# Router logits of three token chunks by row products on VectorE

## The chip, the cores and the metric

One of the eight cores of a Trainium2 chip runs the whole program: TensorE (matrix products), VectorE, ScalarE and GpSimd work on the on-chip memory, and SyncE (SP) issues most of the transfers. Each engine takes its instructions in a fixed order and waits on semaphores for the others. The metric is the time of one execution in microseconds (us), as the device counts it.

## What is computed

Attention of two kinds (on averaged keys and in a local band) over 4 batches, 8 heads, 576 positions and 64 dimensions is added and laid out as 2304 tokens of 512 numbers. A gated feed-forward layer of width 1536 follows, and then a layer of eight experts, of which each token takes one. The part that the change touches, from the reference:

```python
xn = x / (np.linalg.norm(x, axis=-1, keepdims=True) + 1e-06)
en = expert_emb / (np.linalg.norm(expert_emb, axis=-1, keepdims=True) + 1e-06)
logits = xn @ en.T / tau
expert_idx = np.argmax(logits, axis=1)
...
gate_w = probs[np.arange(N), expert_idx]
for e in range(E):
    h = np.maximum(x[mask] @ w1[e], 0.0)
    out[mask] = gate_w[mask, None] * (h @ w2[e])
```

Here `x` is the output of the gated layer, 2304 x 512, and there are 8 embeddings of 512 numbers.

## The kernel before

**Tiling.** The 2304 tokens are worked in nine chunks of 256, each chunk as two tiles of 128 rows (`m` = 0 and 1). For each chunk the gated layer runs over six blocks `p` of 256 hidden units. In a block, TensorE forms gate and value (L963: groups of 24 products with 256 columns), ScalarE the tanh, VectorE the gating (L914, L916) and the low part (L921), and TensorE adds the block to the chunk's output (L995: 512 columns) in a PSUM bank per tile. Every full-precision product is made as three products of high and low parts. While a block's output products run, the next block's or chunk's L963 products stand around them.

**Routing.** When the last block of a chunk is added, `route(c)` and `route_m(c, m, ...)` send the tokens to their experts. For each tile: the row is copied out of PSUM (L1032), its sum of squares formed on ScalarE (L1035), the row transposed in four pieces on TensorE (L1040), copied (L1045), and multiplied with the transposed embeddings `enT` to eight logits per token (L1050), in a PSUM bank `lp`. GpSimd forms the root of the norm (L1058). For both tiles together VectorE scales the logits (L1090), takes maximum and index (L1093, L1095) and writes one-hot rows `oh` (L1097); TensorE counts ranks with them (L1104, L1105), VectorE makes slots (L1108 to L1116), and GpSimd scatters token number and gate weight into the table `tab` (L1123). All of this runs while TensorE already works on the next chunk's L963 products.

**Experts.** Each expert has up to 336 slots in three tiles. The slot table is loaded (L1239, L1244 on SP), the rows gathered (L1258 on GpSimd), transposed on TensorE (L1268), and multiplied with the expert's two layers (L1312, L1322). The first two tiles of expert 0 are gathered before the last chunk is routed, the others after it. The experts' weights are loaded by SP (L1214, L1217) and split into high and low parts (L1197 on ScalarE, L1200 on VectorE).

**Preparation.** `prep_en` loads the eight embeddings (L457), normalises them on VectorE (L468), transposes them on TensorE and leaves them as `enT` (L473). The weights of the gated layer are loaded at L394 and decoded by L405, L413, L416 and L426.

**Order.** The program is written as many small generators. A list scheduler runs them against estimated durations and priorities and so fixes the order of each engine's instructions when the program is built; an instruction's position in its engine's queue depends on it. Tiles come from slot classes (`ps` PSUM banks, `t2` and `sg` rows, `aw` 4 KB-wide work tiles, `w` weights), and a slot that is given back is reused by whoever asks next.

Of the kernel before, what the change touches and what calls it, by code (L numbers as in the profile page):

```python
# [11 lines left out]
F32 = mybir.dt.float32  # L12
# [7 lines left out]
ALU = mybir.AluOpType  # L20
# [4 lines left out]
P = 128  # L25
B, H, S, D = 4, 8, 576, 64
HP = H // 2
DM = H * D
NTOK = B * S
FF = 1536  # L30
E = 8
# [8 lines left out]
NCHUNK = NTOK // CT  # L40
# [25 lines left out]
def t_dve(n): return 62 + 1.045 * n  # L66
# [180 lines left out]
HEAD_P = [0.0, 0.1, 0.2, 0.3, 1.4, 2.2, 3.2, 4.2, 16.0, 17.0, 18.0, 19.0, 36.0, 37.0, 38.0, 39.0]  # L247
NE = 8
EARLY_N = range(NE)
NV = 4  # L250
REST_P = 0.5
NSET = 3
# [4 lines left out]
def build(tc, a):  # L257
    nc = tc.nc
# [22 lines left out]
    def op(eng, ns, prio=None, how=None):  # L281
        return ("op", eng, ns, prio, how)
# [11 lines left out]
    def dma(n):  # L294
        return ("op", "DMA", t_dma(n), None, None)
# [24 lines left out]
    nc.scalar.dma_start(out=tau, in_=a["tau"].to_broadcast([P, 1]))  # L320
    enT = cst.tile([P, KD, E], F32, name="enT")
    x2d = dr.tile([NTOK, DM], F32, name="x2d")
    tab = dr.tile([E * EST, 4], I32, name="tab")
    ovc = cst.tile([P, 1], F32, name="ovc")
    ovm = cst.tile([P, 1], I32, name="ovm")
# [127 lines left out]
    def prep_en():  # L453
        ps = yield ("get", "ps")
        en, junk = t01[:E, 256:768], ps[:E, 0:DM]
        yield dma(E * 2048)
        nc.sync.dma_start(out=en, in_=a["emb"])  # L457
        ss = cst.tile([E, 4], F32, name="ess")
        yield op("ACT", t_act(DM))
        nc.scalar.activation(junk, en, AF.Square, accum_out=ss[:, 0:1])  # L460
        yield op("POOL", 530)
        nc.gpsimd.tensor_tensor(out=ss[:, 1:2], in0=ss[:, 0:1], in1=half[:E, 0:1], op=ALU.pow)
        yield op("DVE", 80, None, True)
        nc.vector.tensor_scalar(out=ss[:, 2:3], in0=ss[:, 1:2], scalar1=1e-6, scalar2=None, op0=ALU.add)
        yield op("DVE", 120)
        nc.vector.reciprocal(ss[:, 3:4], ss[:, 2:3])
        yield op("DVE", 350, None, True)
        nc.vector.tensor_scalar(out=en, in0=en, scalar1=ss[:, 3:4], scalar2=None, op0=ALU.mult)  # L468
        yield op("PE", 340)
        for k in range(KD):  # L470
            nc.tensor.transpose(ps[:, k * E:(k + 1) * E], en[:, k * P:(k + 1) * P], ident[:E, :E])
        yield op("DVE", 110)
        nc.vector.tensor_copy(enT, ps[:, 0:KD * E].rearrange("p (k e) -> p k e", k=KD))  # L473
        sc.put("ps", ps)
        sc.set("en")


    def pget(n=1):

# [545 lines left out]
    def route_m(c, m, sv, lp):  # L1025

        hi = -1.0
        row = yield ("get", "t2")
        yield ("wait", ("x2", c, m))
        xp = x2p.pop((c, m))  # L1030
        eng = yield psum(DM, hi)
        copy[eng](row, xp)  # L1032
        sc.spawn(sc.cur.prio, store_x2(c, m, row))
        yield op("ACT", t_actp(DM) + 110, hi)
        nc.scalar.activation(xp, xp, AF.Square, accum_out=sv[:, 0, m:m + 1])  # L1035
        sc.spawn(sc.cur.prio, route_norm(c, m, sv))
        yield ("lag", SLACK)
        for k in range(KD):
            yield op("PE", 108, hi)
            nc.tensor.transpose(xp[:, k * P:(k + 1) * P], row[:, k * P:(k + 1) * P], ident)  # L1040
        sc.set(("rowT", c, m))
        tcls = "w" if c == NCHUNK - 1 else "t2"
        x2T = last_T[m] if last_T else (yield ("get", tcls))
        eng = yield psum(DM, hi)
        copy[eng](x2T[:, 0:DM], xp)  # L1045
        sc.put(x2cls(c), xp)
        yield ("lag", SLACK)
        yield op("PE", 810, hi)
        for k in range(KD):
            nc.tensor.matmul(lp[:, m * E:(m + 1) * E], x2T[:, k * P:(k + 1) * P], enT[:, k, :],  # L1050
                             start=(k == 0), stop=(k == KD - 1))
        sc.put(tcls, x2T)
        sc.set(("lg", c, m))

    def route_norm(c, m, sv):
# [11 lines left out]
    def route(c):  # L1067
        hi = -1.0
        if c == NCHUNK - 1:
            for m in range(2):  # L1070
                last_T.append((yield ("get", "w")))
        if c > 0:
            yield ("wait", ("tab", c - 1))
        lgt = [gm.tile([P, 2, E], t, tag=nm, name=f"{nm}{c}") for nm, t in
               (("lg", F32), ("oh", F32R), ("t8", F32), ("mx", F32), ("mxi", U32))]
        lg, oh, t8, mx, mxi = lgt
        sv = gm.tile([P, 4, 2], F32, tag="sv", name=f"sv{c}")
        si = gm.tile([P, 2], I32, tag="si", name=f"si{c}")
        yield ("wait", ("x2", c, 0))
        lp = yield ("get", "ps")  # L1080
        for m in range(2):
            if c == NCHUNK - 1:
                sc.spawn(sc.cur.prio, route_m(c, m, sv, lp))
            else:
                yield from route_m(c, m, sv, lp)
        for m in range(2):
            yield ("wait", ("norm", c, m))
            yield ("wait", ("lg", c, m))
        yield op("DVE", 90, hi)
        nc.vector.tensor_tensor(out=lg, in0=lp[:, 0:2 * E].rearrange("p (m e) -> p m e", m=2), in1=b8(sv[:, 3, :]), op=ALU.mult)  # L1090
        for m in range(2):
            yield op("DVE", 75, hi)
            nc.vector.max(out=mx[:, m, :], in_=lg[:, m, :])  # L1093
            yield op("DVE", 150, hi)
            nc.vector.max_index(out=mxi[:, m, :], in_max=mx[:, m, :], in_values=lg[:, m, :])  # L1095
        yield op("DVE", 90, hi)
        nc.vector.tensor_tensor(out=oh, in0=iota8, in1=b8(mxi[:, :, 0]), op=ALU.is_equal)  # L1097
        sc.spawn(sc.cur.prio, route_gate(c, lg, mx, mxi))

        yield ("lag", SLACK)  # L1100
        yield op("PE", 140, hi)
        rp = lp[:, 2 * E:6 * E].rearrange("p (w m e) -> p w m e", w=2, m=2)
        ohf = oh.rearrange("p m e -> p (m e)")
        nc.tensor.matmul(lp[:, 2 * E:4 * E], tri, ohf, start=True, stop=True)  # L1104
        nc.tensor.matmul(lp[:, 4 * E:6 * E], ones, ohf, start=True, stop=True)  # L1105
        bm = lambda x: x.unsqueeze(1).to_broadcast([P, 2, E])
        yield op("DVE", 90, hi)
        nc.vector.tensor_tensor(out=t8, in0=rp[:, 0], in1=bm(base), op=ALU.add)  # L1108
        yield op("DVE", 80, hi)
        nc.vector.tensor_tensor(out=t8[:, 1, :], in0=t8[:, 1, :], in1=rp[:, 1, 0, :], op=ALU.add)  # L1110
        yield op("DVE", 90, hi)
        nc.vector.tensor_tensor(out=t8, in0=t8, in1=oh, op=ALU.mult)
        yield op("DVE", 90, hi)
        nc.vector.tensor_reduce(out=sv[:, 0, :], in_=t8, axis=AX.X, op=ALU.add)
        yield op("DVE", 90, hi, True)
        nc.vector.tensor_copy(si, sv[:, 0, :])  # L1116
        sc.set(("slot", c))
        sc.spawn(sc.cur.prio, route_base(c, lp, rp))
        yield ("wait", ("gate", c))
        for m in range(2):  # L1120
            yield ("lag", 1700 * m)
            yield op("POOL", 1010, hi)
            nc.gpsimd.indirect_dma_start(  # L1123
                out=tab[:, :], out_offset=bass.IndirectOffsetOnAxis(ap=si[:, m:m + 1].bitcast(U32), axis=0),
                in_=mt[:, 2 * c + m, :], in_offset=None, bounds_check=E * EST - 1, oob_is_err=False)
        yield ("lag", 2500)
        sc.set(("tab", c))
# [47 lines left out]
    def open_experts():  # L1175

        for k in range(HP):
            yield ("wait", ("x", NCHUNK - 1, k))
        at.__exit__(None, None, None)
        ep[0] = e2 = pool("e2")  # L1180
        slots("xh", e2, 2, [P, KD, CAP])
        slots("xl", e2, 2, [P, KD, CAP])
        slots("eh", e2, 2, [P, 2, CAP])
        slots("el", e2, 2, [P, 2, CAP])
        slots("xs", e2, 3, [P, DM])
        sc.set("experts")
# [310 lines left out]
    with tc.manual_schedule():  # L1497
        sc.spawn(0, x_slots(), 0.0)
        sc.spawn(0, x_split(1), 0.0)
        sc.spawn(0, fewer_banks(), 0.0)  # L1500
        for n in range(B * HP):
            sc.spawn(HEAD_P[n], heads(n), 0.0)
        sc.spawn(3, small_consts(), 0.0)
        sc.spawn(1000, keep_warm(), 0.0)
        sc.spawn(4, load_weights(), 0.0)
        sc.spawn(0.1, weight_slots(), 0.0)
        sc.spawn(3, prep_en(), 0.0)
        for c in range(NCHUNK):
            if c != 1:
                sc.spawn(c * 10 + 1, x_split(c), 0.0)  # L1510
        sc.spawn(5, gated(), 0.0)
        sc.spawn(NCHUNK * 10, open_experts(), 0.0)
        sc.spawn(NCHUNK * 10 + 4, load_experts(), 0.0)
        sc.spawn(NCHUNK * 10 + 1, all_slots(), 0.0)
        sc.run()
# [120 lines left out]
```

## Time and profile before

| | |
|---|---|
| median of three runs | 879.08 us (877.41 to 879.35) |
| the profiled execution | 879.53 us, of it the span 877.5 us |
| granted TensorE clock, mean | 0.99 |
| TensorE busy | 858.2 us (98%) |
| VectorE busy | 476.2 us (54%) |
| ScalarE busy | 381.2 us (43%) |
| GpSimd busy | 153.0 us (17%) |
| transfers | 88.10 MB, mean 100 GB/s |

The busy times are of one execution on the chip. TensorE's share says that little is left in which it stands; the views by stretch, by wait and by instruction say where that is. Lines are those of the kernel before. In the rows, PE is TensorE, DVE is VectorE, ACT is ScalarE, POOL is GpSimd; an arrow goes from what is read to what is written (`ps<-xhi,w` writes `ps`).

### The profile page before, as it was taken

To read this page: it belongs to the slowest core of one execution; us is meant where nothing else is said; L and a number is where in the kernel's file an instruction comes from. 1 tells how busy PE (TensorE), PEld (TensorE's weight loads), DVE (VectorE), ACT (ScalarE), POOL (GpSimd) and SP (SyncE) were. 2 spreads that over 40 slices of the span, in tenths; PEclk is the share of its full clock that TensorE was granted. 3 is DMA by queue.
4 is the path that set the end of the run, shared out by engine and by line. 5 is a ranking of instruction groups with operands and counts; after the bars stand their busy time and mean duration, and the time that the engine had idled before them with its cause. 6 is when DMAs were issued, how large, how long until landed. Compare 5 with 4: busy or idle time off the path is not lost. (4 is left out here: it accounts for less than half of the span.)

```text
span 877.5 us, 17216 instructions
## 1 busy us (share of the span) xinstructions
PE 858.2 (98%) x6976; PEld 768.3 (88%) x6977; DVE 476.2 (54%) x1132; ACT 381.2 (43%) x914; POOL 153.0 (17%) x163
## 2 busy tenths in 40 slices
PE   9989999999999999999999999999999999999995
PEld 4777889999999999999999999999888888888883
DVE  4799998566564365663342423666455544545210
ACT  3778788444342243341321313345354444445120
POOL 4443300022112010020010000201320330331111
PEclk9899999999999999999999999999999999999998
DMA  8593545102121021120000000453565554453100
GB/s 250 181 320 99 166 161 176 56 27 82 57 80 57 1 63 47 36 76 1 13 13 1 25 1 25 121 190 121 146 201 167 164 193 142 162 191 119 29 27 28
DMA packets 52627, 88.10 MB, mean 100 GB/s; under 512 B 7806, under 2 KB 24574, under 8 KB 52544
## 3 DMA queue, kind: packets, MB, share of 16 engines
q1 hardware_dynamic: 47664, 76.72, 27.8%
q0 software_dynamic: 4160, 9.48, 3.3%
q8 instruction: 55, 0.90, 0.4%
q10 hardware_dynamic: 720, 0.77, 0.3%
q14 instruction: 28, 0.23, 0.1%
HBM read 77.96 MB, written 10.57 MB: 101 GB/s over the span
## 5 line engine op out<-in xcount | busy, mean ns | idle before, releaser
L963 PE MATMUL ps<-xhi,w 128*128 128x256 f32 x1504 | 295.9, 288 | 1.7 <-POOL w L426 1.3
L963 PEld LDWEIGHTS ps<-xhi,w 128*128 128x128 f32 x1504 | 242.2, 191 | 5.4 <-POOL w L426 1.5
L963 PE MATMUL ps<-xlo,w 128*128 128x256 f32 x752 | 212.5, 283 | 0.0
L963 PEld LDWEIGHTS ps<-xlo,w 128*128 128x128 f32 x752 | 144.0, 191 | 1.4
L1312 PE MATMUL ps<-xh,w 128*128 128x336 f32 (+1 forms) x512 | 124.3, 315 | 0.0
L995 PE MATMUL x<-w,hh 128*128 128x512 f32 x384 | 120.8, 396 | 0.0
L914 DVE SCALAR_TENSOR_TENSOR th<-th,ps 128x256 f32<-128x256 f32 x108 | 45.1, 418 | 131.2 <-ACT th L912 130.8
L912 ACT ACTIVATE th<-ps 128x256 f32<-128x256 f32 x108 | 41.0, 380 | 137.4 <-PE ps L963 135.8
L1312 PEld LDWEIGHTS ps<-xh,w 128*128 128x128 f32 x512 | 88.3, 188 | 2.2
L1200 DVE TENSOR_TENSOR w<-w,w 128x1024 fp32r<-128x1024 f32 x64 | 76.6, 1217 | 22.2 <-ACT w L1197 22.1
L1312 PE MATMUL ps<-xl,w 128*128 128x336 f32 (+1 forms) x256 | 79.8, 312 | 0.0
L995 PEld LDWEIGHTS x<-w,hh 128*128 128x128 f32 x384 | 68.4, 189 | 12.2 <-issue 0.4
L1322 PE MATMUL x<-w,eh 128*128 128x512 f32 x248 | 78.0, 396 | 0.0
L995 PE MATMUL x<-w,hl 128*128 128x512 f32 x192 | 74.9, 390 | 0.0
L919 ACT CAST hh<-th 128x256 fp32r<-128x256 f32 x108 | 43.7, 405 | 68.8 <-DVE th L916 68.2
L1298 DVE SCALAR_TENSOR_TENSOR el<-ps,eh 128x336 fp32r<-128x336 f32 (+1 forms) x62 | 30.3, 493 | 79.1 <-ACT eh L1296 78.5
L1296 ACT ACTIVATE eh<-ps 128x336 fp32r<-128x336 f32 (+1 forms) x62 | 27.4, 442 | 90.0 <-PE ps L1312 84.6
L1197 ACT CAST w<-w 128x1024 fp32r<-128x1024 f32 x64 | 65.6, 1045 | 0.0
L1058 POOL TENSOR_TENSOR sv<-sv,half 128x1 f32<-128x1 f32 x18 | 10.4, 577 | 290.5 <-ACT x L1035 285.0
L921 DVE TENSOR_TENSOR hl<-th,hh 128x256 fp32r<-128x256 f32 x94 | 39.7, 424 | 30.9 <-ACT hh L919 30.8
L1322 PEld LDWEIGHTS x<-w,eh 128*128 128x128 f32 x248 | 45.4, 188 | 9.4
L1337 POOL DMA_INDIRECT out<-sg,tb x23 | 23.3, 1012 | 172.3 <-ACT sg L1329 160.7
(257 smaller groups left out, 1391.5 us busy)
## 6 DMA issues: line engine op xcount, KB each, us to landing
w<-w SPq DMA_DIRECT2D x64, 512.0 KB
w<-w_gate SPq DMA_DIRECT2D x10, 512.0 KB
w<-w_val SPq DMA_DIRECT2D x10, 512.0 KB
w<-w_out SPq DMA_DIRECT2D x10, 512.0 KB
w<-qk SPq DMA_DIRECT2D x16, 291.0 KB
aw<-qk SPq DMA_DIRECT2D x16, 291.0 KB
x2d<-sg SPq DMA_DIRECT2D x18, 256.0 KB
w<-vw SPq DMA_DIRECT2D x8, 320.0 KB
```

The lines of the kernel that those rows point to most:

```text
L912: nc.scalar.activation(th, ps[:, 0:CT], AF.Tanh, scale=0.5)
L914: nc.vector.scalar_tensor_tensor(out=th, in0=th, scalar=1.0, in1=ps[:, 0:CT], op0=ALU.add, op1=ALU.mult)
L919: nc.scalar.copy(hh[:, j].bitcast(F32R), th)
L921: on[e].tensor_tensor(out=hl[:, j].bitcast(F32R), in0=th, in1=hh[:, j].bitcast(F32R), op=ALU.subtract)
L963: nc.tensor.matmul(ps[:, o:o + CT], ww[:, k, fs], xx[:, k, :], start=(k == 0 and n == 0), stop=(k == KD - 1 and n == 2))
L995: nc.tensor.matmul(x2p[c, m], l[:, j, ms], r[:, js], start=(p == 0 and j == 0 and n == 0), stop=(p == NFB - 1 and j == 1 and n == 2))
L1197: nc.scalar.copy(hi.bitcast(F32R), raw)
L1200: nc.vector.tensor_tensor(out=lo.bitcast(F32R), in0=raw, in1=hi.bitcast(F32R), op=ALU.subtract)
L1296: nc.scalar.activation(hh[:, j, 0:n].bitcast(F32R), ps[:, 0:n], AF.Relu)
L1298: nc.vector.scalar_tensor_tensor(out=hl[:, j, 0:n].bitcast(F32R), in0=ps[:, 0:n], scalar=0.0, in1=hh[:, j, 0:n].bitcast(F32R), op0=ALU.max ...
L1312: nc.tensor.matmul(ps[:, 0:n], ww[:, k, fs], xx[:, k, 0:n], start=(k == 0 and t == 0), stop=(k == KD - 1 and t == 2))
L1322: nc.tensor.matmul(yt[:m], l, r, start=(first and n == 0), stop=(last and n == 2))
```

## The change

For the chunks 5, 6 and 7 (`ROWS_C`) the logits are no longer formed by TensorE. A new `route_rows` has VectorE multiply the token row tile (128 tokens x 512) with one embedding at a time, which lies in every partition, and sum the products along the row into one column of `lr`: eight instructions per tile, sixteen per chunk. The products themselves go to a half of a fifth work tile, one half for each `m`, that nothing reads. The four transposes, the copy and the logit products of these chunks are left out, and the PSUM bank of the row is given back after the sum of squares. `prep_en` also stores the normalised embeddings to memory (`end`), and a new `prep_rows` loads them, after the last attention head, into four `aw` tiles with the same two embeddings in each of 128 partitions. The bank `lp` is taken in those chunks when the one-hot rows are issued. `open_experts` also waits for the logits of chunk 7, since it closes the pool in which the work tiles lie. Chunks 0 to 4 and 8 are routed as before.

```diff
+ROWS_C = range(5, NCHUNK - 1)
...
+    end = dr.tile([E, DM], F32, name="end")
...
         nc.vector.tensor_scalar(out=en, in0=en, scalar1=ss[:, 3:4], scalar2=None, op0=ALU.mult)
+        nc.sync.dma_start(out=end, in_=en)
...
+    def prep_rows():
+        for n in range(B * HP):
+            yield ("wait", ("done", n))
+        sl = []
+        for _ in range(5):
+            sl.append((yield ("get", "aw")))
+        for i in range(E // 2):
+            yield dma(P * 4096)
+            nc.sync.dma_start(out=sl[i], in_=bass.AP(tensor=end.tensor, offset=end.offset + 2 * i * DM, ap=[[0, P], [1, 2 * DM]]))
+            en_rows.extend((sl[i][:, 0:DM], sl[i][:, DM:2 * DM]))
+        en_rows.extend((sl[4][:, 0:DM], sl[4][:, DM:2 * DM]))
+        sc.set("rows")
...
+        if c in ROWS_C:
+            sc.put(x2cls(c), xp)
+            sc.spawn(sc.cur.prio, route_rows(c, m, row, lp))
+            return
         yield ("lag", SLACK)
         for k in range(KD):
             yield op("PE", 108, hi)
...
+    def route_rows(c, m, row, lp):
+        yield ("wait", "rows")
+        for e in range(E):
+            yield op("DVE", t_dve(DM) + 60, -0.3, True)
+            nc.vector.scalar_tensor_tensor(out=en_rows[E + m], in0=row, scalar=1.0, in1=en_rows[e], op0=ALU.mult, op1=ALU.mult,
+                                           accum_out=lp[:, m, e:e + 1])
+        sc.set(("rowT", c, m))
+        sc.set(("lg", c, m))
...
-        lp = yield ("get", "ps")
+        if c in ROWS_C:
+            lgs = lr = gm.tile([P, 2, E], F32, tag="lr", name=f"lr{c}")
+        else:
+            lp = lr = yield ("get", "ps")
+            lgs = lp[:, 0:2 * E].rearrange("p (m e) -> p m e", m=2)
...
+        if c in ROWS_C:
+            lp = yield ("get", "ps")
         yield ("lag", SLACK)
...
+        for m in range(2):
+            yield ("wait", ("lg", ROWS_C[-1], m))
         at.__exit__(None, None, None)
```

The scheduler sets the order anew, so instructions also move. Lines of the changed kernel are later ones: L963 is now L982, L914, L916 and L921 are L933, L935 and L940, L1104 is L1143, L1268 is L1309, L1312 and L1322 are L1353 and L1363.

TensorE in the kernel before, at the routing of chunk 5: `sg` is the token row and its transposed copy, `xhi`, `xlo` and `w` belong to chunk 6.

```order
L963 MATMUL ps_1_106<-xhi,w_1_146 128x256
L1040 MATMUL x_1_111<-cn,sg_1_102 128x128 x4
L963 MATMUL ps_1_106<-xhi,w_1_145 128x256
...
L963 MATMUL ps_1_106<-xhi,w_1_148 128x256
L1050 MATMUL ps_1_104<-enT,sg_1_103 128x8 x4
L963 MATMUL ps_1_106<-xhi,w_1_147 128x256
...
L963 MATMUL ps_1_107<-xhi,w_2_769 128x256
L1104 MATMUL ps_1_104<-oh_5178,tri 128x16
L1105 MATMUL ps_1_104<-oh_5178,ones 128x16
```

In the changed kernel these four groups (two tiles) are gone, and the L963 products follow one another up to the rank products.

VectorE in the kernel before, at the same routing: `th` and `hl` belong to the gating of chunk 6, `lg` to `oh` to the routing.

```order
L1060 TENSOR_SCALAR sv_5182<-sv_5182,tau 128x1
L916 SCALAR_TENSOR_TENSOR th_1_100<-th_1_100,ps_1_106 128x256
L1062 RECIPROCAL sv_5182<-sv_5182 128x1
L921 TENSOR_TENSOR hl_1_98<-th_1_100,hh_1_96 128x256
L1090 TENSOR_TENSOR lg_5177<-ps_1_104,sv_5182 128x16
L1093 MAX mx_5180<-lg_5177 128x8
L1095 MAX_INDEX mxi_5181<-mx_5180,lg_5177 128x8
L1093 MAX mx_5180<-lg_5177 128x8
L1095 MAX_INDEX mxi_5181<-mx_5180,lg_5177 128x8
L1097 TENSOR_TENSOR oh_5178<-cn,mxi_5181 128x16
L1132 TENSOR_TENSOR lg_5177<-lg_5177,mx_5180 128x16
L914 SCALAR_TENSOR_TENSOR th_1_101<-th_1_101,ps_1_109 128x256
```

VectorE in the changed kernel, the same place: `sg` is the token row, `aw_11` and `aw_10_4880` hold embeddings, `aw_10_4881` is the tile that nothing reads.

```order
L1083 SCALAR_TENSOR_TENSOR aw_10_4881,lr_5204<-sg_1_104,aw_11_4878 128x512
L940 TENSOR_TENSOR hl_1_100<-th_1_101,hh_1_98 128x256
L1083 SCALAR_TENSOR_TENSOR aw_10_4881,lr_5204<-sg_1_104,aw_11_4878 128x512
L933 SCALAR_TENSOR_TENSOR th_1_102<-th_1_102,ps_1_108 128x256
L1083 SCALAR_TENSOR_TENSOR aw_10_4881,lr_5204<-sg_1_104,aw_11_4879 128x512
L935 SCALAR_TENSOR_TENSOR th_1_102<-th_1_102,ps_1_108 128x256
L1083 SCALAR_TENSOR_TENSOR aw_10_4881,lr_5204<-sg_1_104,aw_11_4879 128x512
L940 TENSOR_TENSOR hl_1_100<-th_1_102,hh_1_98 128x256
L1083 SCALAR_TENSOR_TENSOR aw_10_4881,lr_5204<-sg_1_104,aw_10_4880 128x512 x2
L1127 TENSOR_TENSOR lg_5188<-lr_5204,sv_5193 128x16
L1130 MAX mx_5191<-lg_5188 128x8
L1132 MAX_INDEX mxi_5192<-mx_5191,lg_5188 128x8
```

Row products now stand between all of the gating instructions, down to the last one ahead of the scaling of the logits (now L1127); the one-hot rows follow behind all sixteen.

TensorE in the kernel before, at the opening of the experts: `xs` are gathered rows of experts 0 and 1, `eh` and `el` the hidden layer of expert 0; L1433 is the first layer for the third tile of expert 0, of 80 slots.

```order
L1322 MATMUL x_1_110<-w_5_6571,el_1_6168 128x512
L1268 MATMUL ps_1_108<-cn,xs_1_6171 128x80 x4
L1268 MATMUL ps_1_107<-cn,xs_1_6169 128x128 x4
L1433 MATMUL ps_1_106<-w_2_6285,xh_1_6161 80x256
L1433 MATMUL ps_1_106<-w_2_6284,xh_1_6161 80x256
L1433 MATMUL ps_1_106<-w_2_6285,xl_1_6163 80x256
L1433 MATMUL ps_1_106<-w_2_6285,xh_1_6161 80x256
L1433 MATMUL ps_1_106<-w_2_6284,xh_1_6161 80x256
L1433 MATMUL ps_1_106<-w_2_6285,xl_1_6163 80x256
L1268 MATMUL ps_1_105<-cn,xs_1_6170 128x128 x4
```

TensorE in the changed kernel at that place:

```order
L1363 MATMUL x_1_112<-w_5_6555,el_1_6386 128x512
L1309 MATMUL ps_1_108<-cn,xs_1_6389 128x80 x4
L1363 MATMUL x_1_111<-w_5_6555,eh_1_6384 128x512
L1363 MATMUL x_1_111<-w_4_6554,eh_1_6384 128x512
L1363 MATMUL x_1_111<-w_5_6555,el_1_6386 128x512
L1309 MATMUL ps_1_105<-cn,xs_1_6387 128x128 x4
L1363 MATMUL x_1_112<-w_5_6555,eh_1_6384 128x512
L1363 MATMUL x_1_112<-w_4_6554,eh_1_6384 128x512
L1363 MATMUL x_1_112<-w_5_6555,el_1_6386 128x512
L1309 MATMUL ps_1_106<-cn,xs_1_6388 128x128 x4
```

The products of the second layer that stood ahead of the transposes now stand between them; between the rank products of chunk 8 and the first transpose there are 39 of them where there were 48, and 54 of the first layer where there were 51.

## Rows read from the trace of the kernel before

**Rows 1.** The stretch 432 to 490 us: start:end, length, busy time and instructions per engine, clock, DMA.

```profile
432.00:490.00 58.00, 58.00 (x406) 54.37 (x405) 20.08 (x66) 15.85 (x41) 3.14 (x4) 1.00 0.03 10
```

**Rows 2.** TensorE's waits in the whole span: us in total, times, longest; first and third of eleven.

```profile
PE x L378 <- POOL w L374: 2.1, 1, 2.1
...
PE ps L1268 <- DMA xs<-x2d,tb: 1.4, 1, 1.4
```

**Rows 3.** Timeline of TensorE, 432.8 to 450 us: start, length, line, operation, tiles.

```profile
432.80 0.61 PE L995 MATMUL x<-w,hh 128*128 128x512 f32 x2
...
435.52 0.61 PE L995 MATMUL x<-w,hh 128*128 128x512 f32 x2
...
436.91 0.60 PE L1040 MATMUL x<-cn,sg 128*128 128x128 f32 x4
...
437.47 0.28 PE L963 MATMUL ps<-xlo,w 128*128 128x256 f32 x1
...
438.43 0.96 PE L1050 MATMUL ps<-enT,sg 128*128 128x8 f32 x8
...
439.44 0.28 PE L963 MATMUL ps<-xlo,w 128*128 128x256 f32 x1
...
445.77 0.40 PE L963 MATMUL ps<-xhi,w 128*128 128x256 f32 x2
...
449.73 0.40 PE L963 MATMUL ps<-xhi,w 128*128 128x256 f32 x2
```

**Rows 4.** Timeline of VectorE around the decode of a weight block, 145 to 147 us.

```profile
145.32 0.69 DVE L416 SCALAR_TENSOR_TENSOR aw<-aw,sg 128x512 int32<-128x512 int32 x1 [0.22 <-ACT sg L413]
145.93 0.41 DVE L914 SCALAR_TENSOR_TENSOR th<-th,ps 128x256 f32<-128x256 f32 x1
146.26 0.69 DVE L426 TENSOR_TENSOR w<-w,w 128x512 fp32r<-128x512 f32 x1
```

**Rows 5.** Timeline of ScalarE: a sum read out at L1035; a row copy of chunk 5.

```profile
382.21 0.18 ACT L1035 ACTIVATION_READ_ACCUMULATOR x<-x 128x1 f32 x1
382.30 0.36 ACT L600 ACTIVATE aw<-ps,aw 72x144 f32<-72x144 f32 x1
...
435.04 0.59 ACT L1032 COPY sg<-x 128x512 f32<-128x512 f32 x1 [2.01 <-PE x L995]
```

**Rows 6.** Timeline of VectorE: the routing of chunk 5, 443 to 445 us.

```profile
443.62 0.17 DVE L1090 TENSOR_TENSOR lg<-ps,sv 128x16 f32<-128x16 f32 x1 [0.47 <-PE ps L1050]
...
444.65 0.17 DVE L1097 TENSOR_TENSOR oh<-cn,mxi 128x16 fp32r<-128x16 f32 x1
444.74 0.17 DVE L1132 TENSOR_TENSOR lg<-lg,mx 128x16 f32<-128x16 f32 x1
```

**Rows 7.** Timeline of TensorE: rank products and transposes of gathered rows, 552 to 626 us.

```profile
552.98 0.17 PE L1104 MATMUL ps<-oh,tri 128*128 128x16 f32 x1
...
573.43 0.60 PE L1268 MATMUL ps<-cn,xs 128*128 128x128 f32 x4
...
606.51 0.17 PE L1104 MATMUL ps<-oh,tri 128*128 128x16 f32 x1
...
623.96 0.46 PE L1268 MATMUL ps<-cn,xs 80*128 80x80 f32 x4
...
625.83 0.66 PE L1268 MATMUL ps<-cn,xs 128*128 128x128 f32 x4 [1.41 <-DMA xs<-x2d,tb]
```

**Rows 8.** Timeline of GpSimd: expert 0's first two gathers, 566 to 569 us.

```profile
567.03 1.05 POOL L1258 DMA_INDIRECT xs<-x2d,tb  x1 [0.36 <-issue]
568.39 1.01 POOL L1258 DMA_INDIRECT xs<-x2d,tb  x1 [0.30 <-DVE th L916]
```

**Rows 9.** The gathers of L1258, all 24: from issue to landing.

```profile
DMA to landing us min/median/max: 3.4/5.5/5.8
```

**Rows 10.** Timeline of VectorE: embeddings normalised (L468), a weight block read (L405).

```profile
35.80 0.64 DVE L468 TENSOR_SCALAR w<-w,ess 8x512 f32<-8x512 f32 x1
...
48.65 0.41 DVE L405 TENSOR_SCALAR sg<-w 128x512 int32<-128x512 int32 x1
```

More of the change, by code (lines that the diff above doesn't have):

```diff
@@ L475, in prep_en @@
         sc.set("en")
+    en_rows = []
+    def prep_rows():
[10 more added lines that the diff above has]
+        sc.set("rows")
     def pget(n=1):
@@ L1079, in route @@
         yield ("wait", ("x2", c, 0))
-        lp = yield ("get", "ps")
+        if c in ROWS_C:
[3 more added lines that the diff above has]
+            lgs = lp[:, 0:2 * E].rearrange("p (m e) -> p m e", m=2)
         for m in range(2):
             if c == NCHUNK - 1:
-                sc.spawn(sc.cur.prio, route_m(c, m, sv, lp))
+                sc.spawn(sc.cur.prio, route_m(c, m, sv, lr))
             else:
-                yield from route_m(c, m, sv, lp)
+                yield from route_m(c, m, sv, lr)
         for m in range(2):
@@ L1089, in route @@
         yield op("DVE", 90, hi)
-        nc.vector.tensor_tensor(out=lg, in0=lp[:, 0:2 * E].rearrange("p (m e) -> p m e", m=2), in1=b8(sv[:, 3, :]), op=ALU.mult)
+        nc.vector.tensor_tensor(out=lg, in0=lgs, in1=b8(sv[:, 3, :]), op=ALU.mult)
         for m in range(2):
@@ L1507, in build @@
         sc.spawn(3, prep_en(), 0.0)
+        sc.spawn(3, prep_rows(), 0.0)
         for c in range(NCHUNK):
```

## Prediction

> **What bounds the kernel now.** I read the busy time by stretch first. From 432 to 490 us, one chunk and a little more, TensorE is busy for all 58.00 us at a granted clock of 1.00 (the upper level, 2.4 GHz) and VectorE for 20.08 [rows 1]: the place of the change is bound by TensorE, with 38 us of VectorE free. Next the list of TensorE's waits. It has eleven rows in the whole span, the longest 2.1 us, and 8.7 us in all; one belongs to what the change touches, 1.4 us before the transposes of gathered rows at L1268 [rows 2]. So a product taken off TensorE comes off the end, unless TensorE then stands at something that was just in time. Where that is, the timeline tells: for each instruction of the routing I took when TensorE reaches it and when its operand is there.
>
> **Taken off TensorE.** Per 128-token tile, four transposes (L1040) and the logit products (L1050). The transposes start at 436.91 and the second product behind them at 437.47; without them it would start 0.12 after 436.91, so they cost 0.44. The logit products start at 438.43 and the second product behind them at 439.44: 1.01 less 0.12 is 0.89 [rows 3]. The 0.12 is 33 products of 256 columns in 3.96 us, 445.77 to 449.73 [rows 3]. A tile gives 1.33, six tiles **8.0 us**. ScalarE's copies at L1045 go too, off the path.
>
> **Added on VectorE: the price of a row.** Each of the three chunks gets 16 row products of 128x512 with a summed output (new L1083). The trace of before has no VectorE instruction that writes a sum, so the price is bounded. The nearest row is L416, the same instruction on two SBUF tiles of 128x512, without a sum: the next independent instruction starts 0.61 behind it (145.32 to 145.93), and its own time is 0.69 [rows 4]. What reading a sum out adds is seen on ScalarE: a read of the accumulator is a row of its own, 0.18 long, and the next instruction starts 0.09 behind its start [rows 5]. Low end 0.61, if the sum is free; 0.70 with 0.09; high end 0.87, if main part and read follow each other in full (0.69 and 0.18). I take 0.70, because VectorE's own short instructions overlap in the same way: L1097 starts at 444.65 and is 0.17 long, L1132 starts at 444.74 [rows 6].
>
> **Added: a wait on the path.** TensorE stands at L1104 until the one-hot rows (L1097) are there, and VectorE now has the row products queued ahead of those, with the gating of the running block among them (L914, L916, L921, which TensorE's later products need). I replayed both from the start of the first tile's row copy on ScalarE, 435.04 [rows 5].
> - TensorE, chunks 5 and 6: behind that copy come 18 products of 512 columns at 0.227 (432.80 to 435.52 has 12 [rows 3]) and 129 of 256 columns at 0.12, 19.6 us, less the 0.2 by which TensorE was on its way: it is at L1104 at +19.4. In chunk 7 twelve more products stand ahead, so +20.8.
> - VectorE: the first row starts at +0.7. The rest is paced by TensorE's four 24-product groups (2.88 us each), against three rows and three gating instructions of 0.33 (145.93 to 146.26 [rows 4]) for each, 3.1 us. The fourth group ends at +12.7, its gating starts at +13.7, and the last row ends at +17.8. Scaling, maxima and one-hot took 1.20 (443.62 to 444.82 [rows 6]): one-hot at +19.0.
>
> So 0.4 is left in chunks 5 and 6. In chunk 7 the splits of expert weights (L1200, 1.2 us each) lie on VectorE too and it comes out level, 20.9 against 20.8. I take **0.3** for the three. The margin is thin, and this term is the most sensitive: with 0.85 per row the same replay gives a wait of 1.3 per chunk, with 0.91 2.1.
>
> **Added: later at the gathers.** Two places follow the routing at a fixed distance in time (scatter, table, gather), while TensorE now has less work between.
> - In chunk 8, expert 0's first rows: L1104 of chunk 7 stands at 552.98, L1268 at 573.43, 20.4 later [rows 7]. The gathers are issued at 567.03 and 568.39 [rows 8] and land after a median of 5.5 [rows 9], at about 572.5 and 573.9. TensorE will have 99 products of 256 and 33 of 512 columns between, 19.6 us. The first tile is then just there; the second stands 0.4 behind it and its rows come at 20.9: a wait of **1.0** (0 to 2). Its table load (L1239) has three more weight loads ahead of it on SP's queue; they are issued before the scatter is done, so I add nothing.
> - At the opening of the experts: L1104 at 606.51, first L1268 at 623.96, the second at 625.83 after the 1.41 of waiting [rows 2, 7]. The rows land 17.4 and 19.3 behind L1104. TensorE's order now puts 54 first-layer products (0.12) and 39 second-layer ones (0.23) between, about 15.5 us, and one of the tiles that followed back to back gets products in front. Waits of about 1.9, 0.7 and 0.3 stand where 1.4 stood: **1.5** more (0 to 3).
>
> **Edits that cost nothing, and their cover.** The store of the normalised embeddings on SP (new L471) waits for VectorE's L468, 35.80 and 0.64 long, and holds back the weight load behind it to about 36.8. That block is first read at 48.65 [rows 10]; 512 KB in 11.9 us is 43 GB/s, under the mean of the whole span. Were that cover gone, each us late would reach TensorE by way of the decode. The four broadcast loads (new L492, 2 MB) follow the last head, near 396 us, and are first needed near 436. The PSUM bank `lp` is taken later and the token row held longer: both have more tiles than are in use there, I cost nothing. GpSimd's square root of the norm (L1058) runs beside rows on VectorE; it is one instruction per tile, far ahead of L1090.
>
> **Sum.** −8.0 + 0.3 + 1.0 + 1.5 = −5.2. The profiled execution took 879.53 us (span 877.5, the rest around it), which gives 874.3; the median of the three runs is 879.08, 0.45 lower, which gives 873.9. I start from 879.4, between the two, and say **874.2**; the rivals start there too.
>
> **The rivals.**
> - *All of the gain stays* (the gathers come earlier with the shorter program and the replay's margin holds): 879.4 − 8.0 = 871.4. For it: the scatter chains begin as early as the one-hot does. Against it: TensorE already waited 1.4 at the opening [rows 2].
> - *The sum is read out in full behind each row*, 0.87: the replay then gives 1.6 of wait per chunk, 4.8 for three in place of 0.3, 878.7; 876.5 to 880.5 over 0.82 to 0.91. For it: 0.69 and 0.18 are what the rows show as whole durations, and the rows of one tile write one junk tile, each waiting for the one before. Against it: neighbours overlap everywhere else in the trace, and between most rows stands a gating instruction.
> - *VectorE becomes the bound of chunks 5 to 7, and the kernel slower.* If a row runs at half speed, 1.24 (twice 0.62), a group has 4.7 us of VectorE work for 2.88 of products, the one-hot comes at about +26.6, and TensorE stands 7.2 us at L1104 in each chunk: 879.4 − 8.0 + 21.7 + 2.5 = 896. The point from which it decides is 0.89 per row, where three waits of 1.8 eat what is left of the gain. For it: nothing in the trace shows a row with a sum. Against it: L416 has two SBUF inputs and runs 512 elements in 0.61. The Trainium skill (Vector Engine (DVE) Microarchitecture Reference, section 7, points that are easy to get wrong) states a rule of this kind: a scalar-tensor-tensor with two non-bf16 SBUF sources runs at half throughput, since both read ports are taken and none is left for accumulator readback. The trace does not agree for the form without a sum [rows 4], and no row of it shows the form with one. By the rule the time would be near the 896; by the row it is the 874.2.
> - *The late weights cost*: the store or the broadcasts delay a weight block by some us, 881 to 884. Nothing in the list of waits points there.
>
> **How the numbers follow.** Forecast, 872 to 877: 0.55. All gained, 870.5 to 871.9: 0.13. Sum read in full: 0.20. VectorE the bound: 0.07. Late weights: 0.05. The range leaves out the last two: **870.5 to 880.5**. A measurement of this kernel can tell about 0.2% from no change, 1.8 us: faster is below 877.3, which is the forecast, the full gain and a little of the third case, 0.70; within 0.2%, the rest of the third case, 0.18; slower, 0.12.
>
> **What would show it.** Starts of neighbouring rows of L1083 0.70 apart, with no other instruction between, for the price; TensorE without a wait over 0.5 us at the rank products of chunks 5 to 7 (new L1143) for the replay; the distance from one chunk's norm to the next 2.7 us shorter in chunks 5 to 7 for the removed work; waits at the transposes of gathered rows (new L1309) near 1.0 in chunk 8 and near 3 at the opening for the last terms. I am wrong if a row takes over 0.82, if TensorE waits in chunks 5 to 7 for PSUM banks that late gating holds, or if the gathers come later by more than 3 us.

## The result and the profile after

| | before | changed |
|---|---|---|
| median | 879.22 us (877.41 to 879.89, 4 runs) | 869.05 us (866.75 to 870.24, 4 runs) |
| ratio, 95% interval | | 0.9894 (0.9872 to 0.9916) |
| the profiled execution | 879.53 us, span 877.5 | 868.81 us, span 866.6 |
| TensorE busy | 858.2 us | 849.0 us |
| VectorE busy | 476.2 us | 504.9 us |

The kernel became 10.2 us faster; 5.2 were forecast, and the time lies below the range. The gain is larger than the 8.0 us of work that was taken off TensorE, so two questions stand: whether the 8.0 came whole, and where the rest is from.

The stretch 432 to 490 us of the changed kernel (columns as in [rows 1]): TensorE is as full as before at the same clock, VectorE has gone from 20.08 to 32.05 us.

```profile
432.00:490.00 58.00, 58.00 (x406) 54.38 (x405) 32.05 (x108) 16.13 (x42) 4.30 (x6) 1.00 0.05 19
```

First and fifth line of TensorE's list of waits, the changed kernel. None of its eleven lines is at the rank products (now L1143) or at the transposes of gathered rows (now L1309); the 1.4 us of [rows 2] are gone.

```profile
PE x L380 <- POOL w L376: 2.1, 1, 2.1
...
PE ps L635 <- DVE x L872: 0.5, 1, 0.5
```

**The removed work.** The first tile's norm on GpSimd (start, length, instruction) marks where each chunk's routing begins. Before, chunks 5 to 8:

```profile
436.38 0.57 POOL L1058 TENSOR_TENSOR sv<-sv,half 128x1 f32<-128x1 f32 x1 [42.41 <-ACT x L1035]
...
490.14 0.57 POOL L1058 TENSOR_TENSOR sv<-sv,half 128x1 f32<-128x1 f32 x1 [38.13 <-ACT x L1035]
...
543.98 0.57 POOL L1058 TENSOR_TENSOR sv<-sv,half 128x1 f32<-128x1 f32 x1 [38.08 <-ACT x L1035]
...
598.73 0.57 POOL L1058 TENSOR_TENSOR sv<-sv,half 128x1 f32<-128x1 f32 x1 [23.57 <-ACT x L1035]
```

After:

```profile
436.10 0.57 POOL L1091 TENSOR_TENSOR sv<-sv,half 128x1 f32<-128x1 f32 x1 [42.41 <-ACT x L1054]
...
487.22 0.57 POOL L1091 TENSOR_TENSOR sv<-sv,half 128x1 f32<-128x1 f32 x1 [27.17 <-ACT x L1054]
...
538.42 0.57 POOL L1091 TENSOR_TENSOR sv<-sv,half 128x1 f32<-128x1 f32 x1 [27.45 <-ACT x L1054]
...
590.56 0.57 POOL L1091 TENSOR_TENSOR sv<-sv,half 128x1 f32<-128x1 f32 x1 [11.35 <-ACT x L1054]
```

The distances were 53.76, 53.84 and 54.75 us and are 51.12, 51.20 and 52.14: 2.64, 2.64 and 2.61 less. Three chunks give 7.9; the 8.0 came whole.

**The rows on VectorE**, timeline of the changed kernel, chunk 5 (start, length, instruction):

```profile
435.38 0.69 DVE L1083 SCALAR_TENSOR_TENSOR aw<-sg,aw 128x512 f32<-128x512 f32 x1 [2.17 <-ACT sg L1051]
436.00 0.08 DVE L1083 DVE_READ_ACCUMULATOR aw<-sg,aw 128x1 f32 x1
436.12 0.71 DVE L1083 SCALAR_TENSOR_TENSOR aw<-sg,aw 128x512 f32<-128x512 f32 x1
...
439.88 0.67 DVE L1083 SCALAR_TENSOR_TENSOR aw<-sg,aw 128x512 f32<-128x512 f32 x1
440.48 0.09 DVE L1083 DVE_READ_ACCUMULATOR aw<-sg,aw 128x1 f32 x1
440.48 0.42 DVE L935 SCALAR_TENSOR_TENSOR th<-th,ps 128x256 f32<-128x256 f32 x1
...
451.07 0.69 DVE L1083 SCALAR_TENSOR_TENSOR aw<-sg,aw 128x512 f32<-128x512 f32 x1
451.69 0.08 DVE L1083 DVE_READ_ACCUMULATOR aw<-sg,aw 128x1 f32 x1
...
452.83 0.18 DVE L1134 TENSOR_TENSOR oh<-cn,mxi 128x16 fp32r<-128x16 f32 x1
```

A row is two instructions, 0.67 to 0.71 for the product and 0.08 to 0.09 for reading the sum out. The first two rows start 0.74 apart. Where a gating instruction follows (440.48), it starts 0.60 behind the row and at the same time as the read; over the 48 rows, another instruction that needs no sum starts 0.60 to 0.66 behind, most often 0.61, and the next row or the scaling that reads the sums 0.73 to 0.74. The one-hot rows start at 452.83 and are done at 453.01, 18.25 behind the row copy (434.76). TensorE reaches the rank products without idle time ahead of them:

```profile
454.13 0.17 PE L1143 MATMUL ps<-oh,tri 128*128 128x16 f32 x1
```

That is 1.1 us of margin in chunks 5 and 6; in chunk 7 it is 0.6 (one-hot done at 557.35, L1143 at 557.96).

**The opening of the experts** differs most. Ahead of the gathers stands a chain: rank products, two scatters, table loads on SP, gathers. SP's timeline, before first (L1214 and now L1255 load weights, L1244 and now L1285 tables; L1280 at 606.49 loads the table in between):

```profile
616.16 0.37 SPq L1214 DMA_DIRECT2D w<-w  x1
616.58 0.50 SPq L1244 DMA_DIRECT2D tb<-tab  x1
```

```profile
606.10 0.34 SPq L1285 DMA_DIRECT2D tb<-tab  x1
...
606.97 0.46 SPq L1285 DMA_DIRECT2D tb<-tab  x1
607.59 12.96 SPq L1255 DMA_DIRECT2D w<-w  x3
```

Before, a 512 KB weight load stood ahead of the first table load, and it waited for VectorE; after, it stands behind all three. Its wait, from the list of SP's waits between 600 and 640 us of the kernel before (total, times, longest):

```profile
SPq L1214 <- DVE w L1200: 4.2, 1, 4.2
```

GpSimd at that place, second scatter and first gather, before and after:

```profile
612.09 1.30 POOL L1123 DMA_INDIRECT tab<-cn,si  x1 [2.55 <-DMA tab<-cn,si]
620.52 1.51 POOL L1258 DMA_INDIRECT xs<-x2d,tb  x1 [7.12 <-DMA tb<-tab]
```

```profile
602.67 0.99 POOL L1162 DMA_INDIRECT tab<-cn,si  x1 [2.02 <-DMA tab<-cn,si]
608.81 1.00 POOL L1299 DMA_INDIRECT xs<-x2d,tb  x1 [5.16 <-DMA tb<-tab]
```

Counted from the rank products of chunk 8 (606.51 [rows 7], now 597.99):

| behind the rank products | before | changed |
|---|---|---|
| second scatter | 5.58 | 4.68 |
| first table load issued | 10.07 | 8.11 |
| first gather | 14.01 | 10.82 |

The gathers come 3.2 us sooner on that scale: 0.9 of it is there at the second scatter, ahead of SP's loads, and 2.3 comes between scatter and gather. TensorE is at the first tile 15.7 and at the second 16.7 behind the rank products, and finds both there (no idle time noted):

```profile
613.72 0.44 PE L1309 MATMUL ps<-cn,xs 80*128 80x80 f32 x4
...
614.73 0.60 PE L1309 MATMUL ps<-cn,xs 128*128 128x128 f32 x4
```

### The profile page after: what moved, and what is told of

Its sections match the earlier page's. It is cut to its first block, busy times and chain, and to the rows that moved or that the text cites. A ratio compares the mean times of both kernels' runs of the same rounds, so it can differ in the third digit from the quotient of the medians.

```text
span 866.6 us, 17180 instructions
## 1 busy us (share of the span) xinstructions
PE 849.0 (98%) x6904; PEld 759.1 (88%) x6905; DVE 504.9 (58%) x1230; ACT 377.1 (44%) x906; POOL 154.9 (18%) x163
## 5 line engine op out<-in xcount | busy, mean ns | idle before, releaser
L982 PE MATMUL ps<-xhi,w 128*128 128x256 f32 x1504 | 294.0, 288 | 1.7 <-POOL w L428 1.3
L982 PEld LDWEIGHTS ps<-xhi,w 128*128 128x128 f32 x1504 | 242.5, 192 | 5.3 <-POOL w L428 1.5
L982 PE MATMUL ps<-xlo,w 128*128 128x256 f32 x752 | 213.3, 284 | 0.0
L982 PEld LDWEIGHTS ps<-xlo,w 128*128 128x128 f32 x752 | 144.7, 192 | 1.4
L1353 PE MATMUL ps<-xh,w 128*128 128x336 f32 (+1 forms) x512 | 124.3, 315 | 0.0
L933 DVE SCALAR_TENSOR_TENSOR th<-th,ps 128x256 f32<-128x256 f32 x108 | 45.1, 418 | 108.4 <-ACT th L931 106.0
L1353 PEld LDWEIGHTS ps<-xh,w 128*128 128x128 f32 x512 | 88.3, 188 | 2.3
L1353 PE MATMUL ps<-xl,w 128*128 128x336 f32 (+1 forms) x256 | 79.9, 312 | 0.0
L1363 PE MATMUL x<-w,eh 128*128 128x512 f32 x248 | 78.3, 397 | 0.0
L940 DVE TENSOR_TENSOR hl<-th,hh 128x256 fp32r<-128x256 f32 x94 | 39.8, 424 | 24.7 <-ACT hh L938 24.6
L1363 PEld LDWEIGHTS x<-w,eh 128*128 128x128 f32 x248 | 45.2, 188 | 9.0
```

The lines of the kernel that those rows point to most:

```text
L933: nc.vector.scalar_tensor_tensor(out=th, in0=th, scalar=1.0, in1=ps[:, 0:CT], op0=ALU.add, op1=ALU.mult)
L940: on[e].tensor_tensor(out=hl[:, j].bitcast(F32R), in0=th, in1=hh[:, j].bitcast(F32R), op=ALU.subtract)
L982: nc.tensor.matmul(ps[:, o:o + CT], ww[:, k, fs], xx[:, k, :], start=(k == 0 and n == 0), stop=(k == KD - 1 and n == 2))
L1353: nc.tensor.matmul(ps[:, 0:n], ww[:, k, fs], xx[:, k, 0:n], start=(k == 0 and t == 0), stop=(k == KD - 1 and t == 2))
L1363: nc.tensor.matmul(yt[:m], l, r, start=(first and n == 0), stop=(last and n == 2))
```

## Experiments

**Tables first, in the kernel before.** Once the last chunk's slots are known, weight loads wait until the tables are issued:

```diff
                     raw = yield ("get", "w")
+                    if ("slot", NCHUNK - 1) in sc.ev:
+                        yield ("wait", ("tb", 1, 0))
                     yield dma(P * 4096)
```

> The kernel before, with one thing moved: once the slots of the last chunk are known, weight loads on SP wait until the three slot-table loads of experts 0 and 1 are issued; in the kernel before, one 512 KB weight load that waited for VectorE stood ahead of them. Theory A (the surplus of the change over the 8.0 us of removed products comes from the opening of the experts, where the tables are loaded ahead of that weight load): the tables are issued about 1 us sooner and land faster, the 1.4 us wait of TensorE ahead of the second gathered tile goes, 877.5 to 878.2 us. Rival B (the surplus comes from elsewhere, the order on SP has no part in it): the wait stays at 1.4, 879.2 us.

Measured: 877.25 us (12 runs) beside 878.90 of the kernel before; ratio 0.9977 (0.9960 to 0.9993), 1.65 us less and a little more than expected. No wait for gathered rows is left. SP and GpSimd at the opening:

```profile
614.09 0.34 SPq L1246 DMA_DIRECT2D tb<-tab  x1
...
615.50 0.37 SPq L1219 DMA_DIRECT2D w<-w  x1
```

```profile
611.90 1.00 POOL L1123 DMA_INDIRECT tab<-cn,si  x1 [2.86 <-DMA tab<-cn,si]
617.44 1.00 POOL L1260 DMA_INDIRECT xs<-x2d,tb  x1 [4.55 <-DMA tb<-tab]
```

The first gather follows the second scatter by 5.5 us; it was 8.4 in the kernel before. Two weight loads are now behind the tables, at 615.50 and 616.05. The scheduler made the other engines' orders anew too, but TensorE's is the same up to and with the transposes of the first two tiles, between which the wait was. It reaches the first 17.46 us behind the rank products (17.45 in the kernel before) and goes through those of all three tiles without idle time:

```profile
623.46 1.32 PE L1270 MATMUL ps<-cn,xs 80*128 80x80 f32 x12
```

So it is the order on SP that takes this wait away, with all nine chunks routed on TensorE. Of the 1.65, it explains about 1.3 (the table at the end of this section); a few instructions of VectorE and ScalarE have moved from 619 us on, and of TensorE behind the transposes.

**The weight load first, in the changed kernel.** The reverse edit: the table loads wait for the second weight load that is issued after the slots are known.

```diff
                     yield dma(P * 4096)
+                    if ("slot", NCHUNK - 1) in sc.ev:
+                        late.append(0)
+                        if len(late) == 2:
+                            sc.set("late_w")
...
             yield ("wait", ("tab", NCHUNK - 1))
+            yield ("wait", "late_w")
```

> The changed kernel, with one weight load put back ahead of the three table loads at the opening of the experts, as the kernel before had it. Theory A: the gathers come 1 to 2.5 us later, TensorE waits 1 to 3 us at the transposes of the gathered rows, 870.3 to 872 us. Rival B: as the changed kernel, 869.0 us, and no wait there.

Measured: 874.33 us (7 runs), ratio to before 0.9945 (0.9924 to 0.9967). It is 4.6 us under the kernel before of the same runs, where the changed kernel was 10.2 under its own: 5.6 us of the gain are lost, far more than the 1.3 to 3 expected. SP and GpSimd:

```profile
607.75 0.37 SPq L1261 DMA_DIRECT2D w<-w  x1
608.17 0.49 SPq L1292 DMA_DIRECT2D tb<-tab  x1
```

```profile
603.51 0.99 POOL L1162 DMA_INDIRECT tab<-cn,si  x1 [2.03 <-DMA tab<-cn,si]
612.14 1.00 POOL L1306 DMA_INDIRECT xs<-x2d,tb  x1 [7.65 <-DMA tb<-tab]
```

The first gather comes 8.6 us behind the second scatter, 6.1 in the changed kernel. TensorE's waits (L1481 is the first layer of the third tile, L1433 of the kernel before):

```profile
PE ps L1481 <- DVE xl L1323: 1.3, 1, 1.3
...
PE ps L1481 <- ACT xh L1321: 1.0, 1, 1.0
```

The same kernel by stretch; the last three columns are granted clock, DMA share, GB/s:

```profile
616.00:620.00 4.00, 2.21 (x14) 1.38 (x12) 1.45 (x2) 3.12 (x5) 0.13 (x1) 1.00 0.39 115
620.00:624.00 4.00, 3.33 (x20) 3.34 (x21) 1.90 (x4) 0.59 (x1) 2.00 (x2) 0.70 0.21 72
624.00:628.00 4.00, 4.00 (x33) 4.00 (x33) 0.49 (x1) 0.43 (x1) 0.99 (x1) 0.87 0.83 232
```

TensorE idles for 2.5 us between 616 and 621 us, and the granted clock then is at the lower level (1.2 GHz) for part of the next stretches, 0.70 and 0.87 in the mean; the products of 256 columns start 0.21 apart there instead of 0.12. Set against the changed kernel, all that follows the opening stands 5.5 us later, but the rank products of chunk 8 stand 0.8 later already, and those of the first chunk 0.9 (186.95 and 186.04), where the edit has moved nothing: the opening cost 4.7. Of it 2.3 are the two waits and some 1.5 the clock (17 products at 0.09 more); the rest is not told apart.

No wait for gathered rows stands in the list, which is where Theory A put it. The scheduler set TensorE's order anew with the loads: the second-layer products that stand between the transposes in the changed kernel are all ahead of them again, as in the kernel before, so TensorE comes late enough for the rows and then stands at their copies (L1321, L1323). This run therefore prices the opening as a whole, with SP's order and TensorE's, and not SP's alone.

**Store and loads alone**: the rows are left out (`if c in ROWS_C` made false in `route_m` and `route`), while `end` is stored and broadcast.

> The changed kernel with its store of the embeddings and its four broadcast loads, but all nine chunks routed through TensorE as before: no row products. Theory A (store and loads lie under other work): the time of the kernel before, 878.5 to 879.9 us. Rival (the store holds back a weight load on SP and the decode comes late): 881 to 884 us, with a longer wait of TensorE for weights in the first 170 us.

Measured: 878.93 us (10 runs) beside 878.90; ratio 0.9994 (0.9973 to 1.0015). The store and the load behind it on SP:

```profile
35.99 0.29 SPq L471 DMA_DIRECT2D end<-w  x1
36.33 0.36 SPq L396 DMA_DIRECT2D w<-w_out  x1
```

From TensorE's waits, the one for gathered rows:

```profile
PE ps L1309 <- DMA xs<-x2d,tb: 1.4, 1, 1.4
```

The load that was held back to 36.33 makes no longer wait for weights: in the first 180 us one wait is new, 0.4 us for a load of `qk` (L756), and none of the others is over 0.2 longer. The 1.4 us at the opening are as in [rows 2]. The moved queue and the 2 MB cost nothing that can be measured, and they don't bring the tables forward.

**Every row twice**, 16 more per chunk, to see how near VectorE stands to the path:

```diff
             nc.vector.scalar_tensor_tensor(out=en_rows[E + m], in0=row, ..., accum_out=lp[:, m, e:e + 1])
+            nc.vector.scalar_tensor_tensor(out=en_rows[E + m], in0=row, ..., accum_out=lp[:, m, e:e + 1])
```

> The changed kernel with every row product issued twice in a row (same result, 32 more per chunk in all three chunks counted as 16 plus 16), the order of everything else unchanged. Replay with the measured spacings (0.61 ahead of another instruction, 0.73 ahead of a row): a chunk needs 27 us on VectorE from its first row to its one-hot rows, TensorE is at the rank products 18.8 us after that first row; it stands there some 8 us in each of chunks 5 to 7, 893 us. Rival (VectorE is nowhere near the path, since it is 58% busy over the span): 869 to 871 us, no wait at the rank products.

Measured: 902.21 us (one run, with a profile). Waits at the rank products (L1145 here), and the one of chunk 5 in TensorE's timeline:

```profile
PE ps L1145 <- DVE oh L1136: 26.3, 4, 8.7
```

```profile
461.97 0.38 PE L1145 MATMUL ps<-oh,tri 128*128 128x16 f32 x1 [8.61 <-DVE oh L1136]
```

The waits are 8.6 to 8.75 us in each chunk, a little over the 8 of the replay. TensorE's order is that of the changed kernel, instruction for instruction. What the replay lacked is the clock after the waits (columns as above):

```profile
462.00:466.00 4.00, 4.00 (x18) 4.00 (x19) 2.15 (x13) 0.62 (x2) 1.04 (x1) 0.50 0.01 0
...
470.00:474.00 4.00, 4.00 (x36) 4.00 (x35) 0.75 (x2) 0.39 (x1) 0.00 (x0) 1.00 0.00 0
```

At 462 to 466 us TensorE is busy throughout at 0.50, the lower level; by 470 it is back. Set against the changed kernel, the rank products fall back by 8.8 us in chunk 5, 11.7 more in chunk 6, 11.2 in chunk 7 and 2.8 in chunk 8, which has no rows: the waits of 8.6 to 8.75 are followed by losses of 3.1, 2.4 and 2.8 at the lower clock, 8.3 for the three. With the 2 us by which the waits are longer than the replay's 24, that covers the difference between 893 and 902. So VectorE's margin is real but small: an added 10 us per chunk is not free, although VectorE idles for 42% of the changed kernel's span.

**Two chunks, and one chunk**: `ROWS_C = range(5, 7)`, and `ROWS_C = range(7, 8)`.

> Row products for chunks 5 and 6 only; chunk 7 is routed through TensorE again, and the order on SP at the opening of the experts is that of the kernel before (the weight load ahead of the tables). Theory A (2.67 us per chunk from the removed products, and the rest of the gain from the tables going first): 878.9 less 5.3, 873.6 us, and the wait of TensorE for gathered rows at the opening is still there, near 1.4. Rival D (the surplus belongs to the row products, so that the gain of 10.2 is spread over the three chunks): two thirds of it, 872.1 us.

> Row products for chunk 7 only; the order on SP at the opening is that of the changed kernel (tables ahead of the weight load). Theory A: 878.9 less 2.67 less the 1.65 of the tables, 874.6 us, no wait for gathered rows at the opening. Rival D: one third of 10.2, 875.5 us.

Measured beside 878.24 of the kernel before: chunks 5 and 6 873.61 us (9 runs; 0.9950, 0.9930 to 0.9970), chunk 7 alone 873.56 us (11 runs; 0.9947, 0.9929 to 0.9964). With chunks 5 and 6 the gain is 4.6 (2.6 to 6.1), with chunk 7 4.7 (3.2 to 6.2): not two to one, as a gain per row product would be. Two thirds of 10.2 are 6.8, which the first range leaves out; a third, 3.4, is still within the second. With chunks 5 and 6, the wait for gathered rows (total, times, longest):

```profile
PE ps L1309 <- DMA xs<-x2d,tb: 1.7, 3, 1.3
```

With two chunks it stays; with chunk 7 alone none over 0.2 is left. This agrees with the removed work and the order on SP together: 5.3, and 2.7 + 1.65 = 4.3.

**Four chunks**: `ROWS_C = range(4, NCHUNK - 1)`.

> Row products for chunk 4 as well, whose routing lies where the last attention heads end; the broadcast embeddings are there only after the last head. Theory A: another 2.67, 866.4 us, with the one-hot rows of chunk 4 some 20 us later than before and nobody waiting for them. Rival E (rows of two chunks follow each other and VectorE, which still has work of the last heads, gets late for the gating): TensorE waits at the rank products of chunk 4 or 5, 868 to 871 us.

Measured: **865.31 us** (5 runs), ratio 0.9859 (0.9840 to 0.9877): the fastest kernel here, 12.9 us under the kernel before of the same runs. First row and one-hot rows of chunk 4 on VectorE:

```profile
410.90 0.68 DVE L1083 SCALAR_TENSOR_TENSOR aw<-sg,aw 128x512 f32<-128x512 f32 x1
...
425.91 0.17 DVE L1134 TENSOR_TENSOR oh<-cn,mxi 128x16 fp32r<-128x16 f32 x1
```

TensorE reaches the rank products of chunk 4 at 426.43, 38 us later than in the kernel before, and without a wait; the one-hot rows come 39 us later, where some 20 were expected. The fourth line of its waits, which stands at 206 us, long before any row product:

```profile
PE ps L982 <- DVE aw L653: 1.0, 1, 1.0
```

No line of the list is at a rank product or a gathered row. From chunk 4's norm to chunk 8's it is 2.2 us less than in the changed kernel, near the 2.7 expected (0.2 of the rest is a wait for ScalarE at 430 us). The other 1.1 by which its profiled execution is shorter lies ahead of chunk 4's norm, where no row product is.

**All kernels side by side**, from the profiled executions, in us. Chunk 4's norm and chunk 8's are marks as above; the last two columns go to TensorE's last product, and from it to GpSimd's last scatter of results.

| kernel | first on SP | chunk 4's norm to chunk 8's | chunk 8's norm to last product | last product to last scatter |
|---|---|---|---|---|
| before | weight load | 221.2 | 267.9 | 2.26 |
| store and loads alone | weight load | 221.2 | 268.3 | 2.28 |
| before, tables first | tables | 221.3 | 266.6 | 1.84 |
| chunks 5 and 6 | weight load | 216.3 | 268.4 | 1.39 |
| chunk 7 | tables | 218.6 | 267.0 | 1.39 |
| changed (chunks 5 to 7) | tables | 213.3 | 266.2 | 1.39 |
| changed, weight load first | weight load | 213.3 | 270.8 | 1.39 |
| every row twice | tables | 247.7 | 266.2 | 1.39 |
| chunks 4 to 7 | tables | 211.1 | 266.2 | 1.39 |

The first stretch follows the number of chunks with rows: 2.6, 4.9, 7.9 and 10.1 less for one to four. The second is 266.2 to 267.0 in the five kernels with the tables first and 267.9 to 270.8 in the four with the weight load first, however many chunks have rows. The last scatter of results, before and changed (TensorE's last product starts at 866.64 and 856.72):

```profile
868.90 0.92 POOL L1337 DMA_INDIRECT out<-xs,tb  x1 [2.49 <-ACTq L1522]
```

```profile
858.12 0.92 POOL L1378 DMA_INDIRECT out<-xs,tb  x1 [3.14 <-ACT xs L1370]
```

## Why the prediction was wrong

**Right: the removed work.** 1.33 us per tile, 8.0 in all; the spacing of the norms gives 7.9.

**Right within its doubt: the price of a row.** 0.70 was taken between 0.61 and 0.87; it is about 0.61 where another instruction follows and 0.73 to 0.74 where a row does. The read of the sum is an instruction of its own, as on ScalarE in [rows 5], and it runs beside the next one. The replay of TensorE came out to the tenth (+19.4 forecast, 454.13 − 434.76 = 19.4); the one-hot rows came 0.75 sooner than the replay of VectorE had them (+18.25, forecast +19.0), 0.7 sooner in chunk 7. The term of 0.3 us measured 0. The rule quoted in the prediction from the Trainium skill (Vector Engine (DVE) Microarchitecture Reference, section 7), half throughput for two non-bf16 SBUF sources, does not agree with this trace: 512 fp32 elements with a sum take 0.67 to 0.71, the same as [rows 4] without one. The rate is not halved in either: the 256 elements of L914, which has one of its sources in PSUM, stand 0.33 ahead of the next instruction [rows 4], and 512 elements from two SBUF sources 0.61, where half the rate would need about 1.2 (an estimate from these two rows). The rival that rested on its price fell with it, while its mechanism, priced by the replay, is what the doubled rows show.

**Too high: the gathers of chunk 8.** 1.0 was forecast for the second tile, 0 came. TensorE is at the first of the eight transposes at 577.61, 19.6 us behind the rank products, as counted, and goes through them without idle time. The second gather was issued at 572.85, 14.9 behind them (15.4 before), and its rows were there for the fifth transpose, 0.4 later: within 5.2 us, where the median of 5.5 [rows 9] had been taken.

**Wrong, and the cause: the opening of the experts.** The forecast was 1.5 us more waiting; what came is 1.4 less [rows 2], a difference of 2.9 at that term. The step that failed is "The rows land 17.4 and 19.3 behind L1104": it carried the chain from rank products to gathers over as a fixed time. In the changed kernel they are there at 15.7 and 16.7, when TensorE comes. The chain has a queue in it. In the kernel before, the table loads stood on SP behind a weight load that waited for VectorE's L1200; in the changed kernel the scheduler put them ahead, and the first gather came 14.0 us behind the rank products before and 10.8 after. That the queue alone can do this is shown by tables first in the kernel before: the gather comes 11.4 behind, the wait goes, and the time falls by 1.65 us (0.6 to 3.5). The rest of the 3.2 goes with the scatters, the second of which comes 0.9 sooner in the changed kernel; why, no run shows. The weight load first takes 4.7 from the changed kernel at the opening, TensorE's order there being moved too. With that load first the time is 874.33, next to the forecast, but by other terms: the waits stood at the third tile's products, and the clock took a share. Of the rivals, *all of the gain stays* had the right mechanism for this place, gathers that come earlier, but capped the gain at the 8.0. The prediction looked at SP's queue for chunk 8 and for the early store, and not for this place.

**The sum by what was measured.** The profiled execution of the changed kernel spans 10.8 us less than that of the kernel before (the medians differ by 10.2, 7.4 to 11.3). Of the 10.8, 7.9 is the removed work, 1.7 comes between chunk 8's norm and TensorE's last product, where the 1.4 of waiting went, 0.9 comes behind that product, and 0.3 is there at chunk 4's norm already, ahead of the change. Against the forecast of −5.2, the term of 1.5 is off by 3 (it measured −1.4 as a wait, −1.7 as a stretch), the 1.0 and the 0.3 came as nothing, and the end of the program, which had no term, gave 0.9. That last piece is the same in every kernel with row products, whichever order SP has, and 0.4 with tables first in the kernel before. The scheduler's order moved there too: GpSimd's scatter ahead of the last one starts 1.20 us ahead of TensorE's last product before and 2.72 in the changed kernel. No run here shows why, so the cause of this 0.9 stays open.

**Right: the covers.** Store and broadcast have no cost that can be measured (−2.4 to +1.3 us).

## What to carry to other kernels

When a change takes work off the bound engine, the distances between what follows are not constants: look at each chain that runs beside it for in-order queues, and read in the changed program which transfer stands ahead of which. A small load that a chain waits for belongs ahead of a large one that waits for an engine; the edit that did this gave the kernel before 1.65 us. An engine that is half idle over the span can take work off a full one, as long as the new work ends before the next hand-over: here the margin was 0.6 to 1.1 us, and the price of one instruction decided.

## What the runs showed of the hardware

A VectorE product with a summed output (128x512) is followed by a separate read of 0.08 to 0.09 us, and an independent instruction starts at about the same time as that read, so the sum cost nothing where it was followed by other work, and 0.12 us between two rows. After TensorE had waited 8.6 us (the doubled rows) the granted clock was 0.50 for the next 4 us of full work, and after the two waits of 1.0 and 1.3 us at the opening (weight load first) 0.70 and 0.87 in the two stretches behind; one wait of 1.4 us in the kernel before left the clock at 1.00 (624 to 632 us). So a wait on the bound engine can cost more than its length: 8.6 to 8.75 us became 11.0 to 11.7, and 2.3 became some 3.8. At the opening, a 16-byte-per-row table load took 2.4 to 3.4 us from issue to the start of the gather behind it in the five kernels with the tables first (2.7 in the changed kernel), and 3.4 to 4.8 in the four with a 512 KB load issued 0.4 us ahead of it (3.9 in the kernel before).
